# A fused attention, MLP and gated-MLP kernel: the loads of the q and k sums on GpSimd's queue, their decay pieces made early, the low half of v on GpSimd, one subtraction of the mean, and a block's stores on GpSimd's queue

## The chip, the cores and the metric

The kernel runs as one program on one core of a Trainium2 chip. The metric is the device time of one execution in microseconds (us); lower is better.

## What is computed

Three stages follow each other: causal attention with a decay, an MLP behind a layer norm, and an MLP with a spatial gate. Batch 4, 8 heads, 576 positions, head size 64, model width 512, all in float32 at the interface.

```python
def _attn_ref(q, k, v, f):
    scores = scale * np.matmul(q, k.transpose(0, 1, 3, 2))
    cum = np.cumsum(np.log(np.clip(f, 0.0001, 1.0)), axis=-1)
    decay = cum[:, :, :, None] - cum[:, :, None, :]
    scores = np.where(causal, -1000000000.0, scores + decay)
    scores = scores - np.max(scores, axis=-1, keepdims=True)
    attn = np.exp(scores)
    attn = attn / (np.sum(attn, axis=-1, keepdims=True) + 1e-09)
    return np.matmul(attn, v)

def _moe_ref(x, g_ln, w_ch1, w_ch2):
    mu = np.mean(x, axis=-1, keepdims=True)
    var = np.mean((x - mu) ** 2, axis=-1, keepdims=True)
    xn = (x - mu) / np.sqrt(var + 1e-06) * g_ln
    return x + np.maximum(xn @ w_ch1, 0.0) @ w_ch2

def _moe2_ref(x, w_in, w_spatial, b_spatial, w_out):
    h = np.maximum(x @ w_in, 0.0)
    u, v = h[..., :512], h[..., 512:]
    v_n = layer_norm(v)
    v_s = np.einsum('ts,bsd->btd', w_spatial, v_n) + b_spatial[None, :, None]
    return (u * v_s) @ w_out
```

## The kernel before

**Blocks.** The 576 positions of each of the 4 batch rows are cut into queries 0 to 127 (`attention32`, two batch rows at a time, float32), 128 to 255 (`attention1`, also two at a time) and 256 to 575 (`attention`, one row at a time). `BLOCKS` lists the eight pieces in the order in which they are made; each gives a tile xT of 512 features by 256 positions, and a ninth tile collects the last 64 positions of each row. Each tile goes through `prep` (the attention, a store of xT to the DRAM tensor x2_d, and `norm`) and then through `mlp`, whose output is added onto x2_d by GpSimd DMAs that accumulate (L779). From about 624 us on only the third stage (`mlp2`) is left.

**Two halves.** After the first block matmuls take float16 pairs: a number times a power of two is split into a high half h (a rounded copy, made by ScalarE) and a low half l (the remainder, made by VectorE), and a product takes three matmuls. `make16` splits the MLP's weights (L637, L640), `parts16` the values v (L220, L221), `operands` q and k (L318), `mlp` the hidden layer (L754, L758).

**The sums of q and k.** The scale of q and of k in `attention` comes from the sums of their squares. `qknorm` makes them: eight tiles qs, two buffers, each filled by two DMAs on SyncE's queue of 64 partitions each (L268), VectorE squares and sums the q half (L271) and ScalarE the k half (L272). After the last tile a matmul adds over partitions (L275), and a dozen small steps give the scales. Then GpSimd writes the rows that carry the decay into the score matmul: minus eight times the running sum `cum` of the log decay as three float16 pieces each for queries and keys, with rows of a constant `one` beside them (L286 to L293), and one DMA stores them to decay_d (L294). `operands` loads six rows of it for each head (L313).

```
268  nc.sync.dma_start(out=t[64 * u : 64 * u + 64], in_=self.qk[b, h + u : h + 4 : 2, :64]...)
271  nc.vector.tensor_tensor_reduce(out=q, in0=q, in1=q, ...)
272  nc.scalar.activation(k, k, AF.Square, accum_out=ss[:, 1, i : i + 1])
```

**The norm of a block.** `norm` gets the mean of xT by a matmul and subtracts it, one VectorE instruction for each of four feature tiles (L664); it squares on ScalarE (L667), adds the four tiles on GpSimd (L671, L672) and takes their mean by a matmul (L650). From the second block on the subtraction writes xT in place, so it also waits until the store of xT (L1116, on SyncE's queue) has read it.

**What sets the order.** `run` gives every step of every generator a time on a common scale (`events`; the sums stand at `QKS` + `QKN` times i) and calls them in that order. The framework's scheduler then places the instructions on each engine, in a fixed order. An engine runs its own in that order, and a queue issues its DMAs in that order: one that waits holds up all behind it on the same queue.

## Time and profile before

| | us |
|---|---|
| median of 3 runs (821.86 to 824.97) | 823.38 |
| the profiled execution's own time | 820.29 |
| its span, first to last instruction | 818.5 |
| PE (TensorE matmul) busy | 771.9 |
| DVE (VectorE) busy | 568.6 |
| ACT (ScalarE) busy | 527.9 |
| POOL (GpSimd) busy | 86.4 |

The granted TensorE clock was 0.967 of full over the span. Lnnn is a line of the kernel before. "a<-b" is an instruction that writes tile a from tile b; xN counts instructions. An arrow with "DMA qs<-in_qk_dram" in the chain is the time from the issue of that transfer to its landing. SPq is SyncE's queue, which issues most DMAs. Windows are counted from the first instruction.

### The profile page before, as it was taken

To read this page: it belongs to the slowest core of one execution; us is meant where nothing else is said; L and a number is where in the kernel's file an instruction comes from. 1 tells how busy PE (TensorE), PEld (TensorE's weight loads), DVE (VectorE), ACT (ScalarE), POOL (GpSimd) and SP (SyncE) were. 2 spreads that over 40 slices of the span, in tenths; PEclk is the share of its full clock that TensorE was granted. 3 is DMA by queue.
4 is the path that set the end of the run, shared out by engine and by line. 5 is a ranking of instruction groups with operands and counts; after the bars stand their busy time and mean duration, and the time that the engine had idled before them with its cause. 6 is when DMAs were issued, how large, how long until landed. Compare 5 with 4: busy or idle time off the path is not lost.

```text
span 818.5 us, 16434 instructions
## 1 busy us (share of the span) xinstructions
PE 771.9 (94%) x5980; PEld 572.0 (70%) x5980; DVE 568.6 (69%) x1513; ACT 527.9 (64%) x1328; POOL 86.4 (11%) x128
## 2 busy tenths in 40 slices
PE   8899998985898999699999999999999899999998
PEld 7588886874676777377777878744447667768676
DVE  4699599646459999987995984688534573654634
ACT  4787488646638898887885883567325634656543
POOL 2000015001021212301021020100012000000000
PEclk8999999997799999799999999999999999999999
DMA  8789574489967899987796586552005230000101
GB/s 255 204 301 319 171 185 72 66 194 205 215 164 181 170 176 243 189 172 181 147 206 145 122 147 129 171 163 86 1 14 109 66 117 1 30 30 1 59 1 58
DMA packets 166628, 111.84 MB, mean 137 GB/s; under 512 B 106498, under 2 KB 151874, under 8 KB 166516
## 3 DMA queue, kind: packets, MB, share of 16 engines
q1 hardware_dynamic: 160280, 103.86, 52.8%
q0 software_dynamic: 5264, 5.16, 4.7%
q10 hardware_dynamic: 1004, 1.78, 0.8%
q8 instruction: 47, 0.77, 0.4%
q14 instruction: 33, 0.27, 0.1%
HBM read 71.60 MB, written 14.99 MB: 106 GB/s over the span
## 4 chain that ended last, share of the span: by engine, by line
PE 53%; DVE 17%; DMA 14%; issue 7%; ACT 7%; SPq 1%; POOL 0%; DVEq 0%; ACTq 0%; POOLq 0%
PE ph L747 11%; PE acc L732 10%; PE pb L687 8%; PE pb L689 8%; PE pb L688 8%; DMA qs<-in_qk_dram 5%; DVE wt L640 2%; DVE x L318 2%; DMA PT<-P 2%; DVE P L356 2%; DVE sd L339 2%; PE s L732 1%; DMA vr<-in_v_dram 1%; PE av L499 1%; DMA qk<-in_qk_dram 1%
## 5 line engine op out<-in xcount | busy, mean ns | idle before, releaser
L732 PE MATMUL acc<-hh,wt 128*128 128x256 f16 (+2 forms) x960 | 197.9, 298 | 2.3 <-ACT hh L754 2.1
L747 PE MATMUL ph<-xh,wt 128*128 128x256 f16 (+1 forms) x896 | 189.2, 293 | 9.6 <-DVE hl L758 5.1
L747 PEld LDWEIGHTS <-wt 128*128 128x128 f16 x1344 | 131.2, 100 | 59.4 <-issue 16.7
L732 PEld LDWEIGHTS <-wt 128*128 128x128 f16 x1344 | 132.1, 99 | 45.6 <-issue 4.8
L747 PE MATMUL ph<-xl,wt 128*128 128x256 f16 (+1 forms) x448 | 131.1, 293 | 0.0
L732 PE MATMUL acc<-hl,wt 128*128 128x256 f16 (+1 forms) x416 | 116.7, 284 | 0.0
L754 ACT ACTIVATE hh<-ph 128x256 f16<-128x256 f32 (+2 forms) x128 | 50.9, 398 | 51.8 <-PE ph L747 51.5
L298 ACT ACTIVATE P<-sd,st 128x512 f16<-128x512 f32 (+2 forms) x128 | 70.6, 585 | 11.3 <-DVE st L346 10.3
L758 DVE SCALAR_TENSOR_TENSOR hl<-ph,hh 128x256 f16<-128x256 f32 (+1 forms) x112 | 50.4, 453 | 33.0 <-ACT hh L754 32.7
L343 ACT ACTIVATE sd<-sd,st 128x384 f32<-128x384 f32 (+2 forms) x80 | 54.6, 682 | 19.3 <-DVE st L339 18.8
L356 DVE SCALAR_TENSOR_TENSOR P<-sd,st,P 128x384 f16<-128x384 f32 (+2 forms) x96 | 59.1, 634 | 9.6 <-ACT P L298 9.4
L339 DVE CUSTOM_DVE_ANT_0 sd<-s,mask,qkneg 128x384 f32<-128x384 f32 (+2 forms) x80 | 50.7, 639 | 4.5 <-PE s L335 2.9
L335 PE MATMUL s<-x 128*64 128x288 f16 (+5 forms) x256 | 47.6, 330 | 4.5 <-DVE st L339 3.5
L779 POOL DMA_DIRECT2D x_d<-t x36 | 32.5, 1101 | 182.8 <-DVE t L775 151.2
L318 DVE SCALAR_TENSOR_TENSOR x<-qk,qksc,x 64x320 f16<-64x320 f32 x64 | 45.9, 717 | 2.9 <-ACT x L298 1.4
L298 ACT ACTIVATE x<-qk,qksc 128x320 f16<-128x320 f32 x64 | 38.0, 655 | 3.5 <-PE s L335 2.4
L1030 DVE SCALAR_TENSOR_TENSOR u<-pb,wsc,u 128x288 f32<-128x288 f32 x32 | 15.9, 514 | 34.2 <-PE pb L1029 34.2
L689 PE MATMUL pb<-x2h,wih 128*128 128x288 f16 (+2 forms) x144 | 37.8, 273 | 0.0
L688 PE MATMUL pb<-x2l,wih 128*128 128x288 f16 (+2 forms) x144 | 37.8, 273 | 0.0
L687 PE MATMUL pb<-x2h,wil 128*128 128x288 f16 (+2 forms) x144 | 37.8, 273 | 0.0
L687 PE MATMUL pb<-wsh,vl 128*128 128x288 f16 x128 | 36.6, 286 | 0.2 <-DVE x2s L201 0.2
L689 PE MATMUL pb<-wsh,vh 128*128 128x288 f16 x128 | 36.6, 286 | 0.0
(297 smaller groups left out, 1632.2 us busy)
## 6 DMA issues: line engine op xcount, KB each, us to landing
raw<-in_moe_w_ch_dram SPq DMA_DIRECT2D x32, 512.0 KB
qk<-in_qk_dram SPq DMA_DIRECT2D x32, 448.0 KB
qs<-in_qk_dram SPq DMA_DIRECT2D x16, 448.0 KB
vraw<-in_v_dram SPq DMA_DIRECT2D x5, 1024.0 KB
vr<-in_v_dram SPq DMA_DIRECT2D x16, 320.0 KB
x_d<-xT SPq DMA_DIRECT2D x9, 512.0 KB
x_d<-t POOLq DMA_DIRECT2D x36, 128.0 KB, 4.9
out_dram<-o SPq DMA_DIRECT2D x32, 144.0 KB
```

What stands on the lines that cost most here:

```text
L298: self.nc.scalar.activation(out, in_, AF.Copy, scale=scale)
L318: nc.vector.scalar_tensor_tensor(out=t, in0=qk[r, c], scalar=(sk if c.start else sq)[r], in1=x, op0=ALU.mult, op1=ALU.subtract)
L339: nc.vector.tensor_tensor_reduce(out=sd[:M, c0:c1], in0=ps[:M, : c1 - c0], in1=mask, scale=self.qkneg[:M], scalar=3e38 if n == 0 else st[: ...
L343: nc.scalar.activation(sd[:M, :N], sd[:M, :N], AF.Exp, bias=st[:M, n : n + 1], scale=-1.0, accum_out=st[:M, 2:3])
L356: low = nc.vector.scalar_tensor_tensor(out=dl, in0=src, scalar=rs, in1=dh, op0=ALU.mult, op1=ALU.subtract)
L687: first = mm(out, lhsT=al, rhs=bh, start=start, stop=False, **kw)
L688: mm(out, lhsT=ah, rhs=bl, start=False, stop=False, **kw)
L689: mm(out, lhsT=ah, rhs=bh, start=False, stop=stop, **kw)
L732: ins = nc.tensor.matmul(acc[m], lhsT=a, rhs=b, start=bank not in clear, stop=last and e == len(terms) - 1, skip_group_check=True)
L747: ins = nc.tensor.matmul(ph, lhsT=a, rhs=b, start=k == e == 0, stop=k == NK - 1 and e == len(terms) - 1)
L754: relu = nc.scalar.activation(hh, ph, AF.Relu)
L758: nc.vector.scalar_tensor_tensor(out=hl, in0=ph, scalar=0.0, in1=hh, op0=ALU.max, op1=ALU.subtract)
```

## The change

Five edits in one.

- **Sums' loads.** `qknorm` takes eight tiles of a pool of their own with four buffers. One DMA fills a tile, on GpSimd's queue and over all 128 partitions: `pair_of` views the two stored copies of each head so that the second copy of one head and the first of the next stand in 128 consecutive rows. The first four loads are placed at time `QKL` = 0.98, the squares at `QKS` = 1.325 and after (before: loads and squares from 1.12 on); a square is kept behind the last VectorE instruction of `make16` (`marks["made"]`). A later load is issued once the square of the tile four before is made.
- **Decay pieces.** `decays`, at the start of the program, makes the six rows from `cum` and stores them with two GpSimd DMAs. After the sums only the rows of the constant are left: one GpSimd instruction and two DMAs.
- **Low half of v.** In `attention`, and there alone, `parts16` scales vr in place on GpSimd and subtracts h there (`spare`), in place of one VectorE instruction.
- **Mean.** `norm` subtracts the mean in one VectorE instruction over all four tiles, the mean read with a broadcast.
- **Stores.** The store of xT to x2_d goes to GpSimd's queue.

```diff
-QKS, QKN = 1.12, 0.025
+QKL, QKS, QKN = 0.98, 1.325, 0.008
+QKB = 4
...
@@ decays @@
-        cum = self.cum = self.cst.tile([n, S], F32, name="cum")
+        cum = wk.tile([n, S], F32, name="cum")
+        rows = wk.tile([n, 6, S], F16, name="rows")
...
         nc.gpsimd.dma_start(out=self.decay1_d, in_=dec1)
+        nc.gpsimd.tensor_scalar(out=one, in0=cum, scalar1=-8.0, scalar2=1.0, op0=ALU.mult, op1=ALU.mult)
+        for i in range(3):
+            self.copy(1, rows[:, 3 + i], one)
+            if i < 2:
+                nc.gpsimd.tensor_tensor(out=one, in0=one, in1=rows[:, 3 + i], op=ALU.subtract)
+        self.copy(1, rows[:, :3], rows[:, 3:], -1.0)
+        nc.gpsimd.dma_start(out=self.decay_d[:, :3, :QW], in_=rows[:, :3, 2 * P :])
+        nc.gpsimd.dma_start(out=self.decay_d[:, 3:, QW:], in_=rows[:, 3:])
...
@@ parts16 @@
         nc.scalar.activation(h, v, AF.Copy, scale=scale)
-        nc.vector.scalar_tensor_tensor(out=l, in0=v, scalar=scale, in1=h, op0=ALU.mult, op1=ALU.subtract)
+        if spare:
+            self.copy(1, v, v, scale)
+            nc.gpsimd.tensor_tensor(out=l, in0=v, in1=h, op=ALU.subtract)
+        else:
+            nc.vector.scalar_tensor_tensor(out=l, in0=v, scalar=scale, in1=h, op0=ALU.mult, op1=ALU.subtract)
...
@@ qknorm @@
-        n = B * H // 4
+        n = B * NP // 2
+        cm = self.pool("qs")
+        qs = cm.__enter__()
...
+        def load():
+            i = len(tiles)
+            tiles.append(qs.tile([P, 2, C], F32, tag="qs", name="qs", bufs=QKB))
+            b, p = i * 2 // NP, i * 2 % NP
+            nc.gpsimd.dma_start(out=tiles[i], in_=self.pair_of(b)[p : p + 2].rearrange("p r s -> r p s"))
+
+        for i in range(QKB):
+            load()
+        yield
         for i in range(n):
-            t = at.tile([P, 2, C], F32, tag="qs", name="qs", bufs=2)
-            b, h = i * 4 // H, i * 4 % H
-            for u in range(2):
-                nc.sync.dma_start(out=t[64 * u : 64 * u + 64], in_=self.qk[b, h + u : h + 4 : 2, :64].rearrange("p d s -> d p s"))
+            q, k = tiles[i][:, :, :W], tiles[i][:, :, W:]
+            for ins in (nc.vector.tensor_tensor_reduce(out=q, in0=q, in1=q, ...),
+                        nc.scalar.activation(k, k, AF.Square, ...)):
+                self.after(ins, self.marks["made"])
+            if len(tiles) < n:
+                load()
             yield
-            q, k = t[:, :, :W], t[:, :, W:]
-            nc.vector.tensor_tensor_reduce(out=q, in0=q, in1=q, ...)
-            nc.scalar.activation(k, k, AF.Square, ...)
...
         gp, m = nc.gpsimd, B * H
-        c = one[:m]
-        rows = at.tile([m, 6, C], F16, name="drows", bufs=1)
...
-        gp.dma_start(out=self.decay_d, in_=rows)
+        rows = qs.tile([m, 3, S], F16, tag="rows", name="rows", bufs=1)
+        gp.memset(rows, 0.0)
+        gp.tensor_scalar(out=rows, in0=rows, scalar1=one[:m], scalar2=1.0, op0=ALU.add, op1=ALU.mult)
+        gp.dma_start(out=self.decay_d[:, :3, W:], in_=rows)
+        gp.dma_start(out=self.decay_d[:, 3:, :W], in_=rows[:, :, :W])
+        cm.__exit__(None, None, None)
...
+    def pair_of(self, b):
+
+        return self.qk[b].rearrange("(p u) (v d) s -> p (u v d) s", p=NP, v=2)[:, D : 3 * D]
...
@@ attention @@
-            vsc = self.parts16(vr, vp[:, 0], vp[:, 1], b)
+            vsc = self.parts16(vr, vp[:, 0], vp[:, 1], b, True)
...
@@ make16 @@
-            nc.vector.scalar_tensor_tensor(out=l[:, c], in0=src[:, c], ...)
+            self.marks["made"] = nc.vector.scalar_tensor_tensor(out=l[:, c], in0=src[:, c], ...)
...
@@ norm @@
-        for t in range(NK):
-            nc.vector.tensor_tensor(out=c[:, t, :], in0=x[:, t, :], in1=pm, op=ALU.subtract)
+        nc.vector.tensor_tensor(out=c, in0=x, in1=pm.unsqueeze(1).broadcast_to([P, NK, TOK]), op=ALU.subtract)
...
@@ run, prep @@
-            self.nc.sync.dma_start(out=self.rows(self.x2_d, n), in_=xT)
+            self.nc.gpsimd.dma_start(out=self.rows(self.x2_d, n), in_=xT)
...
-        events += [(QKS + QKN * i, -3, i) for i in range(B * H // 4 + 1)]
+        events += [(QKL, -3, 0)] + [(QKS + QKN * i, -3, i + 1) for i in range(B * NP // 2 + 1)]
```

The scheduler reorders around these edits; three places show what the prediction speaks of. In the changed kernel lines are some 20 further on: L1139 is the store of xT, L286 the load of a qs tile, L293 the square of its q half, L664 and L781 the VectorE lines of `make16` and of the hidden layer, L694 and L695 the GpSimd adds of a norm.

**Queues at the sums.** SyncE's queue before, from the store of the third block's xT on; L439 to L441 load the operands of `attention1` for the fourth:

```order
L1116 DMA x_d<-xT 128x4x256
L439 DMA qk<-in_qk_dram 64x768
L440 DMA qk<-decay_d 2x2x384
L441 DMA vr<-in_v_dram 128x2x128
L268 DMA qs<-in_qk_dram 64x2x896 x2
L439 DMA qk<-in_qk_dram 64x768
L440 DMA qk<-decay_d 2x2x384
L441 DMA vr<-in_v_dram 128x2x128
L268 DMA qs<-in_qk_dram 64x2x896 x2
L439 DMA qk<-in_qk_dram 64x768
L440 DMA qk<-decay_d 2x2x384
L268 DMA qs<-in_qk_dram 64x2x896 x2
```

GpSimd's queue with the change, from the first block's store on:

```order
L1139 DMA x_d<-xT 128x4x256
L694 TENSOR_TENSOR sq<-sq 128x512
L695 TENSOR_TENSOR sq<-sq 128x256
L286 DMA qs<-in_qk_dram 128x2x896 x4
L310 MEMSET rows 32x1728
L1139 DMA x_d<-xT 128x4x256
L694 TENSOR_TENSOR sq<-sq 128x512
L695 TENSOR_TENSOR sq<-sq 128x256
L802 DMA x_d<-t 128x256 x4
L286 DMA qs<-in_qk_dram 128x2x896 x4
L1139 DMA x_d<-xT 128x4x256
L694 TENSOR_TENSOR sq<-sq 128x512
```

The loads of qs have left SyncE's queue. Four now stand ahead of the second block's store and norm on GpSimd's, four behind the accumulates of the first MLP (L802) and ahead of the third block's store.

**VectorE at the sums.** Before, squares stand between the score steps (L451) and the low half of the hidden layer (L758) of the fourth block's stretch:

```order
L758 SCALAR_TENSOR_TENSOR hl<-ph,hh 128x256
L221 SCALAR_TENSOR_TENSOR vp<-vr,vsc,vp 128x256
L455 RECIPROCAL st<-st 128x2
L271 ISA qs,qkss<-qs 128x2x320
L271 ISA qkss 128x1
L451 ISA sd,st<-s,mask 128x256
L451 ISA st 128x1
L451 ISA sd,st<-s,mask 128x256
L451 ISA st 128x1
L462 SCALAR_TENSOR_TENSOR P_1689<-sd,st,P_1689 128x2x128 x2
L758 SCALAR_TENSOR_TENSOR hl<-ph,hh 128x256
L271 ISA qs,qkss<-qs 128x2x320
```

With the change the first four stand right behind the last two instructions of `make16`:

```order
L664 SCALAR_TENSOR_TENSOR wt<-wt,w1c 128x512
L664 SCALAR_TENSOR_TENSOR wt<-wt,w2c 128x512
L212 TENSOR_SCALAR vs<-vs 128x1
L293 ISA qs,qkss<-qs 128x2x320
L293 ISA qkss 128x1
L293 ISA qs,qkss<-qs 128x2x320
L293 ISA qkss 128x1
L781 SCALAR_TENSOR_TENSOR hl<-ph,hh 128x256
L293 ISA qs,qkss<-qs 128x2x320
L293 ISA qkss 128x1
L293 ISA qs,qkss<-qs 128x2x320
L293 ISA qkss 128x1
```

Three of the other four stand some 20 rows on, the last six rows behind them:

```order
L293 ISA qs,qkss<-qs 128x2x320
L293 ISA qkss 128x1
L781 SCALAR_TENSOR_TENSOR hl<-ph,hh 128x256
L235 SCALAR_TENSOR_TENSOR vp<-vr,vs,vp 128x256
L293 ISA qs,qkss<-qs 128x2x320
L293 ISA qkss 128x1
L479 RECIPROCAL st<-st 128x2 x2
L781 SCALAR_TENSOR_TENSOR hl<-ph,hh 128x256
L293 ISA qs,qkss<-qs 128x2x320
L293 ISA qkss 128x1
```

All eight squares have moved from the fourth block's `attention1` to the end of the third's; the last four are spread among the hidden layer's low halves, which TensorE waits for.

**GpSimd in `attention`.** Before, in the fifth block (x<-x is the copy of half of an operand that `operands` makes, L300, and MEMSET P clears padding):

```order
L350 MEMSET P_2880 128x2x64
L779 DMA x_d<-t 128x256 x4
L300 TENSOR_SCALAR x_3178<-x_3177 64x320
L350 MEMSET P_3164 128x2x64
L300 TENSOR_SCALAR x_3570<-x_3569 64x320
L300 TENSOR_SCALAR x_3581<-x_3580 64x320
L300 TENSOR_SCALAR x_3670<-x_3669 64x320
```

With the change, at the same place:

```order
L320 TENSOR_SCALAR vr<-vr,vsc 128x640
L233 TENSOR_TENSOR vp<-vr,vp 128x640
L802 DMA x_d<-t 128x256 x2
L320 TENSOR_SCALAR x_3168<-x_3167 64x320
L320 TENSOR_SCALAR x_3558<-x_3557 64x320
L802 DMA x_d<-t 128x256 x2
L374 MEMSET P_3153 128x2x64
L320 TENSOR_SCALAR vr<-vr,vsc 128x640
L233 TENSOR_TENSOR vp<-vr,vp 128x640
```

Two instructions on vr have come ahead of the accumulates and of the copies; there are sixteen such pairs in the program.

## Rows read from the trace of the kernel before

**Rows 1.** The page, part 4: the chain that ended last, by line.

```profile
PE ph L747 11%; PE acc L732 10%; PE pb L687 8%; PE pb L689 8%; PE pb L688 8%; DMA qs<-in_qk_dram 5%; DVE wt L640 2%; DVE x L318 2%; DMA PT<-P 2%; DVE P L356 2%; DVE sd L339 2%; PE s L732 1%; DMA vr<-in_v_dram 1%; PE av L499 1%; DMA qk<-in_qk_dram 1%
```

**Rows 2.** Four stretches: length, PE, PEld, DVE, ACT, POOL busy (count), clock, DMA, GB/s.

```profile
...
100.00:140.00 40.00, 36.28 (x278) 30.36 (x277) 38.54 (x99) 34.69 (x89) 13.74 (x13) 0.96 0.68 143
140.00:168.00 28.00, 27.94 (x285) 23.61 (x286) 17.94 (x59) 17.23 (x55) 0.00 (x0) 1.00 0.35 66
168.00:228.00 60.00, 45.02 (x301) 33.34 (x299) 32.54 (x106) 35.99 (x100) 5.55 (x6) 0.80 1.06 206
...
240.00:330.00 90.00, 86.79 (x788) 66.89 (x786) 83.22 (x214) 76.08 (x195) 17.15 (x29) 1.00 0.93 196
...
```

**Rows 3.** The chain in order of time, 140 to 250 us (start, length, what).

```profile
...
166.03 0.37 SPq L1116
...
169.02 6.78 DMA qs<-in_qk_dram
...
177.81 9.55 DMA qs<-in_qk_dram
...
189.52 11.90 DMA qs<-in_qk_dram
...
204.12 7.99 DMA qs<-in_qk_dram
...
217.81 6.57 DMA qs<-in_qk_dram
...
```

**Rows 4.** Waits, 168 to 228 us (total, times, longest).

```profile
...
DVE qs L271 <- DMA qs<-in_qk_dram: 23.1, 8, 4.4
ACT qs L272 <- DMA qs<-in_qk_dram: 16.3, 8, 3.6
...
```

**Rows 5.** Instructions on tile qs alone: length, DVE busy, ACT busy, clock, DMA, GB/s.

```profile
168.00:228.00 60.00, 6.61 (x8) 10.06 (x16) 0.80 1.06 206
```

**Rows 6.** The chain in order of time: a 448 KB load onto 128 partitions.

```profile
275.48 4.59 DMA qk<-in_qk_dram
```

**Rows 7.** DVE groups by form, 119.8 to 126.9 us: count, busy us, mean ns.

```profile
L640 DVE SCALAR_TENSOR_TENSOR wt<-wt,w1c 128x512 f16<-128x512 f32 x4 | 3.0, 744 | 0.0
L640 DVE SCALAR_TENSOR_TENSOR wt<-wt,w2c 128x512 f16<-128x512 f32 x3 | 2.2, 746 | 0.0
```

**Rows 8.** The same two groups, 126.9 to 134.3 us.

```profile
L640 DVE SCALAR_TENSOR_TENSOR wt<-wt,w1c 128x512 f16<-128x512 f32 x3 | 3.5, 1157 | 0.0
L640 DVE SCALAR_TENSOR_TENSOR wt<-wt,w2c 128x512 f16<-128x512 f32 x3 | 3.3, 1100 | 0.0
```

**Rows 9.** POOL alone, 126.9 to 135.3 us: length, busy, clock, DMA, GB/s.

```profile
126.90:135.30 8.40, 7.83 (x7) 0.85 0.35 69
```

**Rows 10.** POOL groups by form over the whole run.

```profile
...
L290 POOL TENSOR_TENSOR dcum<-dcum,drows 32x576 f32<-32x576 f32 x2 | 2.9, 1432 | 0.2
...
L286 POOL TENSOR_SCALAR dcum<-cum 32x576 f32<-32x576 f32 x1 | 0.7, 696 | 0.1
...
```

**Rows 11.** DVE groups by form over the whole run.

```profile
...
L221 DVE SCALAR_TENSOR_TENSOR vp<-vr,vsc,vp 128x640 f16<-128x640 f32 x16 | 14.2, 890 | 2.1 <-ACT vp L220 1.9
...
L664 DVE TENSOR_TENSOR xT<-xT,av 128x256 f32<-128x256 f32 x28 | 9.9, 413 | 4.9 <-DMA x_d<-xT 2.6 <-PE ph L747 2.1
...
L681 DVE TENSOR_TENSOR xT<-xT,y 128x1024 f32<-128x1024 f32 x8 | 9.7, 1216 | 0.0
...
L664 DVE TENSOR_TENSOR xT<-xT,s 128x256 f32<-128x256 f32 x8 | 2.8, 416 | 1.6 <-PE s L650 0.8 <-DMA x_d<-xT 0.8
...
```

**Rows 12.** Tile x_d: duration ns min/median/max, first and last start; landing.

```profile
...
L779 POOL DMA_DIRECT2D x_d<-t x36: 858/905/1738, 122.5 to 622.8; - x36
...
DMA to landing us min/median/max: 3.0/4.9/8.1
```

**Rows 13.** The chain in order of time at the end of the fifth block.

```profile
...
316.69 4.92 DMA x_d<-xT
...
```

**Rows 14.** Timeline, 323 to 343 us: GpSimd add of the squares, and its idle time.

```profile
...
324.32 1.69 POOL L671 TENSOR_TENSOR sq<-sq 128x512 f32<-128x512 f32 x1 [9.13 <-ACT sq L667]
...
```

More of the change, by code (lines that the diff above doesn't have):

```diff
@@ L263, in qknorm @@
         self.qkneg = self.cst.tile([P, 1], F32, name="qkneg")
[L264 to L268 removed]
+        tiles = []
+        def load():
[6 more added lines that the diff above has]
+        yield
+        for i in range(n):
+            q, k = tiles[i][:, :, :W], tiles[i][:, :, W:]
+            for ins in (nc.vector.tensor_tensor_reduce(out=q, in0=q, in1=q, scale=1.0, scalar=0.0, op0=ALU.mult, op1=ALU.add, accum_out=ss[:, 0, i : i + 1]),
+                        nc.scalar.activation(k, k, AF.Square, accum_out=ss[:, 1, i : i + 1])):
+                self.after(ins, self.marks["made"])
+            if len(tiles) < n:
+                load()
             yield
[L270 to L272 removed]
         nc.vector.tensor_reduce(out=tot, in_=ss, axis=mybir.AxisListType.X, op=ALU.add)
@@ L282, in qknorm @@
         gp, m = nc.gpsimd, B * H
-        c = one[:m]
-        rows = at.tile([m, 6, C], F16, name="drows", bufs=1)
-        t = at.tile([m, S], F32, name="dcum", bufs=1)
-        gp.tensor_scalar(out=t, in0=self.cum, scalar1=-8.0, scalar2=1.0, op0=ALU.mult, op1=ALU.mult)
-        for i in range(3):
-            self.copy(1, rows[:, 3 + i, W:], t)
-            if i < 2:
-                gp.tensor_tensor(out=t, in0=t, in1=rows[:, 3 + i, W:], op=ALU.subtract)
-        self.copy(1, rows[:, :3, :W], rows[:, 3:, W + 2 * P :], -1.0)
-        gp.tensor_scalar(out=rows[:, :3, W:], in0=rows[:, 3:, W:], scalar1=0.0, scalar2=c, op0=ALU.mult, op1=ALU.add)
-        gp.tensor_scalar(out=rows[:, 3:, :W], in0=rows[:, :3, :W], scalar1=0.0, scalar2=c, op0=ALU.mult, op1=ALU.add)
-        gp.dma_start(out=self.decay_d, in_=rows)
+        rows = qs.tile([m, 3, S], F16, tag="rows", name="rows", bufs=1)
[4 more added lines that the diff above has]
+        cm.__exit__(None, None, None)
     def copy(self, e, out, in_, scale=1.0):
@@ L639, in make16 @@
                 self.after(ins, self.xh)
-            nc.vector.scalar_tensor_tensor(out=l[:, c], in0=src[:, c], scalar=sc, in1=h[:, c], op0=ALU.mult, op1=ALU.subtract)
+            self.marks["made"] = nc.vector.scalar_tensor_tensor(out=l[:, c], in0=src[:, c], scalar=sc, in1=h[:, c], op0=ALU.mult, op1=ALU.subtract)
     def pair(self, j):
```

6 lines of the change are left out of this document (2 added, 4 removed).

## The prediction

> **What bounds the kernel now.** I read the page's busy table first: TensorE is busy for 771.9 of 818.5 us, so a gain must come from a place where TensorE waits or crawls. The chain that ended last is the second view [rows 1]. Matmul lines fill most of it; among the rest one entry is larger than every other, 5% of the span for the landing of qs, the loads for the sums of q and k. The third view, busy time by stretch, shows where [rows 2]. From 140 to 168 us TensorE makes 285 matmuls in 28 us at full clock, 10.2 per us, and this is the pace at which it has no gaps. From 168 to 228 us it makes 301 in 60 us, at a mean granted clock of 0.80 of full. At the earlier pace these take 301 / 10.2 = 29.6 us, so this stretch loses 60 - 29.6 = 30.4 us. Neither VectorE (32.5 of 60) nor ScalarE (36.0) is full there, but the DMA engines are (share 1.06, against 0.35 just before).
>
> The chain in order of time names the mechanism [rows 3]. At 166.03 the SyncE queue issues the third block's store, and from 169.02 on five landings of qs follow each other, 6.78 + 9.55 + 11.90 + 7.99 + 6.57 = 42.8 us of the 60. With two buffers a load waits for a square, and the square, in VectorE's and ScalarE's fixed order, holds up the low halves that TensorE needs. The waits agree: eight of VectorE for 23.1 us and eight of ScalarE for 16.3 [rows 4]. In 240 to 330 us the limits differ: VectorE is busy for 83.2 of 90 us and TensorE for 86.8 [rows 2], so there both are close to the bound.
>
> **The change, part by part.** The sum is made against the profiled execution, 820.29 us; the median of the runs shown is 3.1 us above it.
>
> *1. The stall goes.* The eight loads leave the stretch, and its loss of 30.4 us is the most that can come back: -30.4. The squares go too, 6.61 us of VectorE and 10.06 of ScalarE [rows 5]. They move mostly into 140 to 168 us, where VectorE has 10.1 and ScalarE 10.8 us free [rows 2]; this is their cover, and without it they would cost up to 10 us.
>
> *2. What is late next there.* The fourth block's `attention1` remains: 32.54 - 6.61 = 25.9 us of VectorE and 35.99 - 10.06 = 25.9 us of ScalarE, feeding each other. If they overlap fully, TensorE's 29.6 us bound the stretch, and nothing is given back. If they alternate strictly, it lasts 51.9 us, and 22 are given back. From 100 to 140 us the same two engines do 38.5 and 34.7 us of work in 40 [rows 2], so they overlap well; I am nearer the good end and take +10 (0 to 22).
>
> *3. The loads at their new place.* They are 8 x 896 KB = 7.3 MB. At the 206 GB/s of the full stretch that is 36 us of all engines; free are 0.32 x 40 + 0.65 x 28 = 31 us between 100 and 168 [rows 2], so they almost fit. The first four can land before about 140 us, when `make16` ends. The last four can only be issued behind the first squares, some 18 us of transfers into 65% free engines, so the last may land 27 us later, while the order wants it after about six steps of the hidden layer, 6 x 24 / 10.2 = 14 us. The wait lies between 0 and 13 us. One load is twice the 448 KB that took 4.59 us on 128 partitions [rows 6], about 9 us, against some 4 us of VectorE work between the fourth square and the fifth; I take +5. GpSimd's part is cheap: it is idle from 140 to 168 us [rows 2], and an issue of 128 rows costs it 0.9 us [rows 12].
>
> *4. Decay pieces.* GpSimd worked for 7.83 us between 126.9 and 135.3 us [rows 9], in a stretch in which VectorE is busy for 38.5 of 40. The low halves of `make16`, 744 and 746 ns just before [rows 7], took 1157 and 1100 ns beside it [rows 8]: 3 x 0.413 + 3 x 0.354 = 2.3 us lost, or 0.29 us of VectorE per us of GpSimd. At the program's start GpSimd has nothing else to do and the rows are not needed until after 228 us, so this is free there: -2 (-3 to 0).
>
> *5. Low half of v.* VectorE loses sixteen instructions, 14.2 us [rows 11]. GpSimd gets sixteen pairs; by the nearest rows, 1432 and 696 ns for 576 columns [rows 10], a pair of 640 columns costs 2.13 x 640 / 576 = 2.36 us, together 37.8. GpSimd has the time (17.2 of 90 us busy [rows 2]), and the product with v comes a pair of heads later, so 1.5 us more of delay is hidden. The price is contention: 0.29 x 37.8 = 11 us of VectorE, bounded by 0 and 37.8. The Trainium skill, page "SBUF — State Buffer", section "Who interferes with whom", says that a VectorE instruction with two SBUF inputs and a GpSimd instruction that reads SBUF exclude each other, and that the loser blocks fully. Taken at its hardest this charges all 37.8 us; rows 7 to 9 show the effect, at 0.29.
>
> *6. One subtraction.* 36 instructions, 9.9 + 2.8 us, become nine of 1024 columns. The nearest is the 1216 ns of the product of the same size [rows 11]: 9 x 1.22 = 10.9, a gain of 1.8 us. Parts 5 and 6 change VectorE by -14.2 + 11 - 1.8 = -5 us (-16 to +22). TensorE is at 96% there, so I count nothing: 0 (-4 to +22).
>
> *7. Stores.* On GpSimd a store has 512 rows, by 0.9 us for 128 rows between 0.9 and 3.6 us, nine times. The adds of the same block stand behind it; in the fifth block they began at 324.32 [rows 14], 7.6 us after the store's issue at 316.69 [rows 13], and this covers it. The in-place subtraction waits for the store to be read: 4.92 us there [rows 13], against 3.0 to 8.1 for GpSimd's quarter-sized accumulates [rows 12]. What is queued behind a late store or a late vr on GpSimd is the operand copy of a next head. I take +1 (-2 to +6).
>
> Sum: -30.4 + 10 + 5 - 2 + 0 + 1 = -16.4, so 803.9 us for an execution like the profiled one and **807 us** for the median.
>
> **Rivals.** *Late squares.* Parts 1 and 2 go as I say, but the last four loads land at the bad end, +13 instead of +5. For it speaks that they share the DMA engines with the fourth block's operands; against it that those engines are at 0.35 before 168 us. That gives 815 us.
>
> *Nothing won.* The stretch is then held by VectorE and ScalarE alternating, +22, with a wait of 7 us for the squares: -30.4 + 22 + 7 - 2 + 1 = -2.4, 821 us. The DMA bytes do not change, and from 100 to 228 us the engines have 0.68 x 40 + 0.35 x 28 + 1.06 x 60 = 101 of 128 us to do already. The Trainium skill, page "DMA: Bandwidth & Descriptors", section "Issuing engines are not separate DMA queues", says that another queue saves only the time of issuing, since all share the same sixteen engines. By that rule alone the new queue wins nothing and only the earlier start counts; no row here shows two queues loading at once.
>
> *GpSimd blocks VectorE.* The place is 240 to 480 us, the price up to 1 us of VectorE per us of GpSimd: 37.8 - 16 = +22 on an engine that is 92% busy, 807 + 22 = 829 us, slower than before. It decides above (16.4 + 16) / 37.8 = 0.86. For it speaks that VectorE there mostly runs instructions of two SBUF inputs; against it the 0.29 of rows 7 to 9, measured beside such instructions too.
>
> **How the numbers follow.** About 0.5%, 4 us, is what a measurement of this kernel can tell from no change. The forecast has 0.61 and its own range is 795 to 817 us; late squares 0.12, faster as well; nothing won 0.14; GpSimd blocking 0.13. So faster has 0.73, the same 0.14, slower 0.13. The range reaches from 794, about halfway from the sum to its good ends in parts 2 to 7, to 824, which takes in late squares and nothing won; outside are GpSimd blocking and some 0.05 below.
>
> **What would show it.** Right: no landing of qs on the chain for more than some 8 us together; the matmuls that now run from 168 to 228 us done in some 40 to 47 us at a clock near full; landings of the last four loads before 170 us. Low halves of v and operand copies on GpSimd should leave the mean of VectorE's `P` and `x` lines (L356, L318) up by under a tenth. Wrong: a wait of VectorE for qs of over 10 us, VectorE's two-input lines up by a fifth or more between 240 and 480 us, or a norm that waits for GpSimd's store.

## The result and the profile after

The changed kernel takes 831.16 us (median of 5 runs, 828.85 to 833.09) against 823.38 for the kernel before: ratio 1.0088, 95% interval 1.0066 to 1.0111. It is slower, and the prediction of 807 us, with a range to 824, was wrong. The profiled execution took 831.16 us, its span is 829.4 us (before 818.5), and the granted TensorE clock was 0.969.

Line numbers of the changed kernel are 10 to 14 higher in `parts16` and 18 to 24 higher from `qknorm` on: L380 is the `P` line (before L356), L342 the `x` line (L318), L486 the `P` of `attention1` (L462), L495 its product with v (L471), L687 the mean subtraction (L664), L781 the hidden layer's low half (L758).

Busy time by stretch after the change; columns as in [rows 2]:

```profile
20.00:40.00 20.00, 14.62 (x77) 10.70 (x77) 11.72 (x24) 14.46 (x29) 3.50 (x4) 0.84 0.74 191
40.00:100.00 60.00, 58.94 (x383) 50.24 (x381) 47.58 (x81) 40.89 (x82) 3.99 (x4) 0.99 0.93 323
100.00:140.00 40.00, 35.63 (x256) 29.70 (x254) 30.06 (x91) 28.20 (x76) 6.37 (x7) 0.91 0.61 160
140.00:168.00 28.00, 25.56 (x231) 21.93 (x232) 24.86 (x71) 27.49 (x71) 2.97 (x4) 1.00 0.39 111
168.00:228.00 60.00, 42.58 (x377) 33.51 (x375) 33.91 (x112) 32.74 (x100) 9.53 (x10) 0.86 0.81 136
228.00:240.00 12.00, 12.00 (x124) 10.22 (x122) 5.78 (x10) 5.61 (x12) 2.54 (x4) 1.00 0.65 223
240.00:330.00 90.00, 85.08 (x760) 64.62 (x758) 84.09 (x206) 75.57 (x197) 30.49 (x39) 1.00 0.87 180
330.00:360.00 30.00, 26.43 (x265) 19.62 (x264) 29.15 (x77) 24.75 (x66) 10.66 (x14) 1.00 1.02 174
360.00:480.00 120.00, 113.10 (x1036) 89.48 (x1034) 97.69 (x230) 86.94 (x227) 36.15 (x45) 0.99 0.74 153
480.00:530.00 50.00, 47.55 (x425) 38.72 (x425) 30.05 (x74) 25.78 (x65) 6.10 (x9) 0.97 0.64 138
```

Three stretches of the kernel before that [rows 2] leaves out:

```profile
330.00:360.00 30.00, 21.88 (x183) 14.55 (x182) 28.32 (x73) 25.44 (x67) 6.92 (x10) 0.77 0.92 174
360.00:480.00 120.00, 117.06 (x1097) 92.31 (x1094) 102.90 (x265) 92.09 (x243) 20.57 (x32) 1.00 0.78 164
480.00:530.00 50.00, 50.00 (x459) 41.07 (x458) 29.87 (x78) 25.39 (x61) 1.59 (x4) 1.00 0.65 151
```

TensorE's matmuls, the counts in the first brackets, tell where the time went. (They are of unequal lengths, so 10 to the microsecond is rough.) In 168 to 228 us it makes 377 where it made 301: part of the old stall is gone. But from 100 to 168 it makes 487 where it made 563, and these 76 cancel those 76. From 240 to 330 it makes 28 fewer; from 330 to 360, 82 more (a stall of the kernel before is gone there); from 360 to 530, 95 fewer. By 240 us the changed kernel has made 1448 since 20 us and the old one 1481, 33 more: nothing is won there, and more is lost after 360.

The stall between 168 and 228 us has become one idle time. First what TensorE did (start, length, what, in brackets the idle time before it and what ended it), then the waits from 168 to 228 us:

```profile
170.58 0.27 PE L755 MATMUL acc<-hh,wt 128*128 128x256 f16 x1
181.42 0.85 PE L495 MATMUL av<-PT,vp 128*64 128x128 f16 x12 [10.56 <-DMA PT<-P]
```

```profile
POOL x_d L1139 <- ACT xT L496: 26.7, 1, 26.7
...
PE av L495 <- DMA PT<-P: 11.4, 2, 10.6
...
DVE qs L293 <- DMA qs<-in_qk_dram: 6.0, 2, 4.7
```

TensorE waits for a transposed P, that is, for a DMA, and not for a square. VectorE's waits for qs are down from 23.1 us [rows 4] to 6.0. The last four loads were issued between 158.72 and 164.61 us, behind squares that came after the last weight of `make16` (156.8 us).

After 240 us two VectorE groups are slower and GpSimd has new ones (page, part 5, and the groups by line from 230 to 530 us; busy us, mean ns, idle time before):

```profile
L380 DVE SCALAR_TENSOR_TENSOR P<-sd,st,P 128x384 f16<-128x384 f32 (+2 forms) x96 | 66.9, 718 | 16.3 <-ACT P L318 15.9
L342 DVE SCALAR_TENSOR_TENSOR x<-qk,qksc,x 64x320 f16<-64x320 f32 x64 | 49.9, 779 | 1.7
```

```profile
L233 POOL TENSOR_TENSOR vp<-vr,vp 128x640 f16<-128x640 f32 x16 | 24.8, 1552 | 1.1
...
L320 POOL TENSOR_SCALAR vr<-vr,vsc 128x640 f32<-128x640 f32 x16 | 13.7, 854 | 52.7 <-ACT st L369 24.0 <-ACT vp L230 20.6 <-PE ph L770 5.2
```

Before, `P` took 634 ns and `x` 717. GpSimd's pair takes 1.55 + 0.85 = 2.41 us (2.36 were forecast), and its queue stands still for 52.7 us in front of the scaling.

### The profile page after: what moved, and what is told of

Read it like the earlier page. It is cut to its first block, busy times and chain, and to the rows that moved or that the text cites. A ratio compares the mean times of both kernels' runs of the same rounds, so it can differ in the third digit from the quotient of the medians.

```text
span 829.4 us, 16441 instructions
## 1 busy us (share of the span) xinstructions
PE 769.7 (93%) x5980; PEld 572.4 (69%) x5980; DVE 568.9 (69%) x1470; ACT 527.4 (64%) x1328; POOL 137.1 (17%) x180
## 5 line engine op out<-in xcount | busy, mean ns | idle before, releaser
L318 ACT ACTIVATE P<-sd,st 128x512 f16<-128x512 f32 (+2 forms) x128 | 70.4, 585 | 16.2 <-DVE st L370 7.2
L380 DVE SCALAR_TENSOR_TENSOR P<-sd,st,P 128x384 f16<-128x384 f32 (+2 forms) x96 | 66.9, 718 | 16.3 <-ACT P L318 15.9
L781 DVE SCALAR_TENSOR_TENSOR hl<-ph,hh 128x256 f16<-128x256 f32 (+1 forms) x112 | 50.4, 452 | 35.4 <-ACT hh L777 35.3
L802 POOL DMA_DIRECT2D x_d<-t x36 | 33.7, 1089 | 122.5 <-DVE t L798 102.7
L342 DVE SCALAR_TENSOR_TENSOR x<-qk,qksc,x 64x320 f16<-64x320 f32 x64 | 49.9, 779 | 1.7
L770 PE MATMUL ph<-xg,wt 128*128 128x256 f32 x128 | 34.4, 404 | 5.0 <-ACT xg L734 4.6
L318 ACT ACTIVATE x<-qk,qksc 128x320 f16<-128x320 f32 x64 | 37.7, 655 | 1.4 <-PE s L359 1.4
L523 PE MATMUL av<-PT,vp 128*64 128x320 f16 (+2 forms) x480 | 32.3, 270 | 5.6 <-DMA PT<-P 4.8
```

Source lines behind the costliest of these rows:

```text
L318: self.nc.scalar.activation(out, in_, AF.Copy, scale=scale)
L342: nc.vector.scalar_tensor_tensor(out=t, in0=qk[r, c], scalar=(sk if c.start else sq)[r], in1=x, op0=ALU.mult, op1=ALU.subtract)
L380: low = nc.vector.scalar_tensor_tensor(out=dl, in0=src, scalar=rs, in1=dh, op0=ALU.mult, op1=ALU.subtract)
L770: ins = nc.tensor.matmul(ph, lhsT=a, rhs=b, start=k == e == 0, stop=k == NK - 1 and e == len(terms) - 1)
L781: nc.vector.scalar_tensor_tensor(out=hl, in0=ph, scalar=0.0, in1=hh, op0=ALU.max, op1=ALU.subtract)
```

## Experiments

Each kernel was timed beside the kernel before; the ratio is to that. "Loads alone" is the kernel before with the sums' loads and the early decay pieces of the change.

| label | what it is | us | ratio (95%) |
|---|---|---|---|
| u_store | changed, stores back on SyncE | 827.61 | 1.0045 (1.0023, 1.0066) |
| u_v | changed, low half of v back on VectorE | 816.58 | 0.9924 (0.9900, 0.9948) |
| u_sub | changed, four subtractions | 820.41 | 0.9952 (0.9933, 0.9972) |
| loads_alone | loads and decay pieces only | 802.12 | 0.9744 (0.9724, 0.9764) |
| l_sub | loads alone + one subtraction | 812.95 | 0.9878 (0.9839, 0.9918) |
| l_store | loads alone + stores on GpSimd | 812.90 | 0.9875 (0.9852, 0.9899) |
| l_v | loads alone + low half of v on GpSimd | 821.38 | 0.9979 (0.9956, 1.0001) |
| a_nosq | changed, last four squares left out | 833.08 | 1.0117 (1.0089, 1.0145) |
| l_dummy | loads alone + GpSimd pairs that serve nothing | 823.18 | 1.0019 (0.9994, 1.0043) |
| l_vfree | l_v, the pair fed from tiles of its own | 806.92 | 0.9821 (0.9798, 0.9843) |
| l_early | loads alone, squares early | 799.39 | 0.9732 (0.9694, 0.9770) |
| e_sub | l_early + one subtraction | 808.43 | 0.9811 (0.9796, 0.9827) |
| e_store | l_early + stores on GpSimd | 808.20 | 0.9818 (0.9789, 0.9848) |
| a_early | changed, squares early | 818.17 | 0.9935 (0.9912, 0.9957) |
| e_two | l_early, two subtractions | 808.30 | 0.9843 (0.9798, 0.9887) |
| e_rev | l_early, four in reverse sequence | 802.44 | 0.9757 (0.9725, 0.9790) |
| b_decay | before + early decay pieces | 821.91 | 1.0011 (0.9988, 1.0035) |
| b_shape | before, loads over 128 partitions | 812.42 | 0.9905 (0.9876, 0.9935) |

### Which part costs

```diff
u_store:  -nc.gpsimd.dma_start(out=self.rows(self.x2_d, n), in_=xT)
          +nc.sync.dma_start(out=self.rows(self.x2_d, n), in_=xT)
u_v:      -vsc = self.parts16(vr, vp[:, 0], vp[:, 1], b, True)
          +vsc = self.parts16(vr, vp[:, 0], vp[:, 1], b)
u_sub:    -nc.vector.tensor_tensor(out=c, in0=x, in1=pm.unsqueeze(1).broadcast_to(...), op=ALU.subtract)
          +for t in range(NK):
          +    nc.vector.tensor_tensor(out=c[:, t, :], in0=x[:, t, :], in1=pm, op=ALU.subtract)
loads_alone: all three
```

> The changed kernel with the stores of a block's attention output back on SyncE's queue; everything else as changed. Theory A (the store stands in GpSimd's queue among the loads, so the second block's mean subtraction slid from 102.4 us to 116.8, the last weights from about 145 to 157 us, and with them the squares and the last four loads; this made TensorE's idle time of 10.6 us at 170 to 181): the subtraction starts before 106 us again, the first square before 148, the idle time is under 4 us, and the time is 815 to 821. Theory B (the loads come in two halves and the second half is late wherever the store is): the idle time stays at 7 to 11 us and the time is 827 to 832. Theory C (GpSimd's new work on v slows VectorE after 240 us): says nothing of the stretch before 240 us, and expects the loss of about 9 us between 240 and 530 us to stay.

> The changed kernel with the low half of v back on VectorE; everything else as changed. Theory C (GpSimd's work beside VectorE's two-input instructions costs more than the 14.2 us it takes off VectorE): the means of the lines that make P and x fall from 718 and 779 ns back to 630 to 650 and 715 to 730, and the time is 820 to 824. Rival to C (VectorE's loss and gain cancel, and the loss after 240 us is GpSimd's order: copies and stores wait behind v): the means fall the same, the time is 826 to 829. Theories A and B: nothing changes before 230 us, the idle time at 170 to 181 stays.

> The changed kernel with the mean subtracted in four instructions again; everything else as changed. All theories: 830 to 834, at most 2 us slower than the changed kernel. If a single subtraction that waits for the whole mean and the whole store were what holds the norms, it would be faster, under 827.

> The kernel before with only the new loads for the sums on GpSimd's queue, in two halves of four, and the decay pieces made early; the stores, the low half of v and the subtractions are as before. Theory A: the stretch from 140 to 240 us gains what the prediction gave it, 805 to 812. Theory B: TensorE still stands idle for 7 to 11 us before the last squares, 816 to 822. If parts 1 and 4 win nothing by themselves: 822 to 826.

The loads and the decay pieces alone give 802.12 us, 21 us less than before, 5 less than my forecast for the whole, and below every range that I gave this run. The other three edits cost 29 us together; undoing one gives back 3.5, 14.6 and 10.7. In u_sub the theories expected nothing; what came is the alternative named beside them, under 827. Theory A was half right. With the stores on SyncE the last four loads go out from 148.1 us instead of 158.7, but TensorE's idle time stays (8.4 us, ended by PT again) only 13 us earlier, as theory B says. In loads_alone no wait for PT there is longer than 1.7 us. For the low half of v the two lines fell about as theory C said (`P` 627 ns, `x` 742, both just outside its ranges), with a larger gain than it said (816.58 against 820 to 824).

Then one edit at a time on top of the loads:

> The new loads and early decay pieces (802.1 us by themselves) and, of the other three edits, the single subtraction alone. Additive costs (each edit costs what undoing it gave back: 3.5 for the stores, 10.7 for the subtraction, 14.6 for the low half of v; their sum, 28.8, is the whole distance from 802.1 to 831.2): 812 to 814. Theory D (the subtraction itself costs nothing; it moves the order so that a transpose of P by DMA is in flight together with the last loads for the sums, and both crawl; in the changed kernel the DMA engines then moved about 100 GB/s at a full share): between 802 and 813, and the excess over 802 stands as idle time of TensorE between 150 and 175 us, in front of a product that waits for PT.

> The new loads and early decay pieces and, of the other three edits, the stores on GpSimd's queue alone. Additive costs: 805 to 806.5. Theory A (a store behind loads moves the second block's norm and the squares by 10 us): the first square at 155 to 160 us instead of 147, the second block's subtraction after 110 us, and the time is 804 to 812.

> The new loads and early decay pieces and, of the other three edits, the low half of v on GpSimd alone. Additive costs: 815 to 818. Theory C (contention: undoing it took 37.4 us of GpSimd and left VectorE 3.1 us less busy although it got 14.2 us of work back, so 17.3 / 37.4 = 0.46 us of VectorE per us of GpSimd): VectorE's P line back at 690 to 730 ns against 627, its x line at 760 to 790 against 706, the loss lies after 240 us, and the time is 810 to 818. If the loss came from the order of the other edits: 801 to 805.

They cost 10.8, 10.8 and 19.3 us. The sum, 40.9, is more than the 29.0 that they cost together: they overlap. In l_sub TensorE waits 9.9 us for a PT, from 160.5 to 170.4 us, as theory D says; the time alone would fit additive costs too. l_v is slower than both of its ranges, and its lines are above theory C's (`P` 737 ns, `x` 806). In l_store the last loads go out from 160.6 us, as theory A says, without one long wait (812.9 us, just above its range).

### What the last loads meet

a_nosq is the changed kernel with the last four loads made and their squares left out:

```diff
-for ins in (nc.vector.tensor_tensor_reduce(...), nc.scalar.activation(k, k, AF.Square, ...)):
+for ins in () if i >= QKB else (nc.vector.tensor_tensor_reduce(...), nc.scalar.activation(k, k, AF.Square, ...)):
```

> The changed kernel, in which the last four loads for the sums are made as before but their squares are left out (the sums take in the first four loads alone). Theory D (the transposes of P and the last loads slow each other): TensorE's idle time of about 10 us near 175 us stays, 6 us or more, and while the two overlap the DMA engines move under 200 GB/s at a share over 0.9; 825 to 831. Rival, theory E (VectorE's fixed order: the squares that wait for the loads hold up P, 4.7 us, and the rest follows from it): with no square behind these loads the idle time is under 3 us and the time is 817 to 823.

The idle time stays, and the time is 833.1 us, above the range of theory D, so VectorE's sequence (theory E) is not its cause. TensorE's long wait in a_nosq from 155 to 190 us, and the busy times by 5 us (the last three numbers of a row are clock, DMA share and GB/s):

```profile
PE av L495 <- DMA PT<-P: 10.9, 1, 10.9
```

```profile
160.00:165.00 5.00, 4.55 (x42) 3.92 (x41) 3.75 (x21) 5.00 (x19) 1.96 (x3) 1.00 0.99 348
165.00:170.00 5.00, 5.00 (x48) 4.47 (x47) 2.21 (x7) 1.67 (x6) 0.00 (x0) 1.00 1.32 252
170.00:175.00 5.00, 0.65 (x6) 0.33 (x4) 0.00 (x0) 0.00 (x0) 0.00 (x0) 0.81 1.04 128
175.00:180.00 5.00, 0.00 (x0) 0.00 (x0) 0.00 (x0) 0.00 (x0) 0.00 (x0) 0.50 1.18 73
```

The loads begin at 348 GB/s. Once transposes are in flight with them, the DMA engines are at a full share and move 73 to 128. The same stretch of the changed kernel, then the stretch of loads_alone in which its last loads run:

```profile
170.00:175.00 5.00, 0.85 (x8) 0.52 (x6) 1.81 (x5) 1.26 (x2) 0.00 (x0) 0.99 1.26 89
175.00:180.00 5.00, 0.00 (x0) 0.00 (x0) 0.15 (x1) 0.00 (x0) 0.00 (x0) 0.50 0.96 122
```

```profile
155.00:160.00 5.00, 5.00 (x48) 4.47 (x46) 4.62 (x19) 4.25 (x14) 0.00 (x0) 1.00 1.00 375
160.00:165.00 5.00, 4.50 (x49) 3.66 (x47) 3.50 (x12) 5.00 (x15) 0.00 (x0) 1.00 0.80 106
```

In loads_alone the first transpose that meets these loads is issued at 155.21 and the last load has landed by 162.1, so the two are in flight together for 6.9 us at most. The queues tell it as well. From 150 to 170 us, first u_store, then loads_alone (queue, packets, MB, share; q0 carries the loads, q1 mostly the transposes, in u_store one load of 128 KB as well):

```profile
q0 software_dynamic: 557, 3.55, 61.1%
q1 hardware_dynamic: 1784, 0.51, 50.3%
```

```profile
q0 software_dynamic: 562, 3.57, 46.2%
q1 hardware_dynamic: 3693, 0.92, 37.9%
```

A packet of q1 costs 50.3% of 16 x 20 us / 1784 = 90 ns in u_store, 33 ns in loads_alone. a_nosq shows it within one run. From 145 to 155 us transposes alone are in flight (but for one packet of another queue), from 170 to 180 transposes and loads:

```profile
q1 hardware_dynamic: 2112, 0.52, 27.3%
```

```profile
q1 hardware_dynamic: 983, 0.25, 77.4%
q0 software_dynamic: 119, 0.76, 33.7%
```

By the same sum a transpose's packet takes 21 ns alone and 126 ns beside loads. So loads and transposes in flight together slow each other: that is shown. Why they do so no row here tells. The Trainium skill, page "SBUF — State Buffer", section "Who interferes with whom", has another reason for a stalled DMA of GpSimd's queue: a VectorE instruction that holds the port which GpSimd needs to write the descriptors. It is not that here, since VectorE is busy for 0.00 us from 170 to 180 us in a_nosq.

### The low half of v: contention or waiting

```diff
l_dummy:  vsc = self.parts16(vr, vp[:, 0], vp[:, 1], b)
         +self.copy(1, d32, d32, vsc)
         +nc.gpsimd.tensor_tensor(out=d16[:, 1], in0=d32, in1=d16[:, 0], op=ALU.subtract)
l_vfree:  the same two, out=vp[:, 1] in the second, and no low half on VectorE
```

> The new loads and early decay pieces (802.1 us), with the low half of v on VectorE as before, and beside it on GpSimd sixteen pairs of instructions of the same shapes as the low half's (a scaling of 640 columns and a subtraction), on a tile of their own; they wait for no other engine's work and nobody waits for them. The low half on GpSimd cost 19.3 us. Theory C (contention, 0.44 us of VectorE per us of GpSimd): VectorE's P line at 700 to 740 ns, its x line over 760, VectorE busy for 14 to 18 us more than with the loads alone, and the time is 812 to 825, since nothing is taken off VectorE here. Rival, theory F (the loss is waiting: GpSimd's queue stands still for ScalarE's high half, 82 us in all, and operand copies wait behind it): the P line rises as well, but the time is 802 to 808.

> The new loads and early decay pieces; VectorE's sixteen low halves of v are left out, and GpSimd writes that half from tiles of its own, in two instructions of the same shapes that do not wait for ScalarE's high half or for the load of v. So the low half of v is not computed here. GpSimd's work by itself, beside a VectorE that keeps its low halves, cost 21 us; the real low half on GpSimd costs 19.3 although it takes 14.2 us off VectorE. Theory C (only VectorE's busy time counts): 21 less 14, 805 to 811. Theory F (what counts is also that the queue waits for ScalarE and operand copies wait behind it): the same, since the waits are gone here, while the real low half cost 10 to 14 us more for its waits. If it comes out at 816 to 823 instead, the busy time taken off VectorE is worth nothing there and the price is the longer single instruction in each chain.

The first row of the page for loads_alone, l_v, l_dummy and l_vfree, in this order:

```profile
PE 765.5 (96%) x5980; PEld 570.4 (71%) x5980; DVE 566.6 (71%) x1513; ACT 526.5 (66%) x1328; POOL 94.0 (12%) x139
```

```profile
PE 774.1 (94%) x5980; PEld 572.7 (70%) x5980; DVE 570.1 (69%) x1497; ACT 527.4 (64%) x1328; POOL 133.8 (16%) x171
```

```profile
PE 769.3 (94%) x5980; PEld 570.0 (70%) x5980; DVE 585.1 (71%) x1513; ACT 526.2 (64%) x1328; POOL 142.1 (17%) x179
```

```profile
PE 764.2 (95%) x5980; PEld 568.7 (71%) x5980; DVE 574.9 (71%) x1497; ACT 527.0 (65%) x1328; POOL 143.3 (18%) x179
```

In l_dummy 48.1 us more of GpSimd make VectorE 18.5 us busier: 0.38 us per us. In l_vfree it is 8.3 + 14.2 (the low halves that VectorE no longer makes) = 22.5 for 49.3, 0.46; in l_v 3.5 + 14.2 = 17.7 for 39.8, 0.44. This is contention, and with nothing taken off VectorE the pairs cost 21.1 us of time, so theory F alone is out. (In l_dummy the pairs bunch, as they wait for little: GpSimd is busy for 38.9 of the 60 us from 240 to 300 us, against 18.4 in l_v. The 21.1 us are their price at that place.)

But it is not what l_v costs: there VectorE is only 3.5 us busier, and the time is 19.3 longer. In l_vfree VectorE is 8.3 us busier, and the time is only 4.8 longer. What l_vfree lacks are the waits for ScalarE's high half and for the load of v, and GpSimd's work on vr. So about 14.5 of the 19.3 us go with these, and theory C does not cover them. (The three differ in the order of the program too, which by the next section can be worth some microseconds; the split is no finer than that.) The rows of l_v, 230 to 530 us:

```profile
L380 DVE SCALAR_TENSOR_TENSOR P<-sd,st,P 128x384 f16<-128x384 f32 (+2 forms) x96 | 68.7, 737 | 11.9 <-ACT P L318 11.2
```

```profile
L320 POOL TENSOR_SCALAR vr<-vr,vsc 128x640 f32<-128x640 f32 x15 | 13.3, 890 | 96.1 <-ACT vp L230 44.3 <-ACT st L369 37.9 <-issue 9.2
```

GpSimd's queue stands for 96 us in front of the scaling of v, and what is behind it in that queue (operand copies of later heads, sums of squares of the norm) stands too. But a standing queue is not yet a cost. In loads_alone it stands just as long, 96.4 us, in front of the operand copies, and in l_vfree the subtraction waits too, for TensorE to release vp:

```profile
L560 POOL TENSOR_TENSOR vp<-d,d 128x640 f16<-128x640 f32 x14 | 22.7, 1621 | 54.2 <-PE av L522 54.2
```

TensorE's own waits from 230 to 530 us add up to 7.8 us in loads_alone, 14.0 in l_vfree and 20.7 in l_v. Two of l_v:

```profile
PE s L359 <- DVE st L363: 7.9, 8, 2.4
...
PE s L359 <- POOL vr L320: 3.3, 1, 3.3
```

Little of this is a direct wait for GpSimd. There is also a rival to theory F that no run tests: vr has one buffer, and in l_v the next load of v waits four times, 7.5 us, until GpSimd's subtraction has read it; in loads_alone it waits once, 2.0 us, for VectorE's. So the 14.5 us are shown as the price of tying the pair to ScalarE, to the load and to vr; how it reaches TensorE stays open.

### Where the squares stand, and what an order costs

```diff
l_early, a_early, e_*: -QKL, QKS, QKN = 0.98, 1.325, 0.008
                       +QKL, QKS, QKN = 0.98, 1.0, 0.008
                       -self.after(ins, self.marks["made"])
e_sub, e_store:        the edit of l_sub, of l_store
```

> The new loads and early decay pieces, with the squares put before the last weights instead of behind them, so that the last four loads are issued between about 105 and 125 us. Theory D (loads and transposes of P in flight together slow each other): the first attention with transposes runs there too, so the collision moves to 105 to 135 us; TensorE, which still has other work there until 125, loses under 5 us, and the time is 798 to 806. If the late squares are what is left of the loss between 140 and 240 us: 792 to 798. If the 6.6 us of squares on a full VectorE before the last weights count fully: 806 to 810.

> Early squares (799.4 us) with the single subtraction. With late squares this edit cost 10.8 us, and TensorE stood idle from 158 to 168. Theory D (it cost that because the order let the last loads meet transposes of P): with the loads over by 135 us nothing is left to collide, 797 to 802. If the single subtraction costs by itself (a norm that waits for the whole sum): 806 to 811.

> Early squares (799.4 us) with the stores on GpSimd's queue. With late squares this edit cost 10.8 us: 7 of them before 240 us, without a single long idle time. Theory A (it cost that because a store behind the loads moved the second block's norm): the loads are still in that queue, so 804 to 811. If it cost only through the place of the squares: 798 to 803.

> The whole changed kernel (831.2 us) with early squares. Theory D: TensorE's idle time of 10.6 us at 170 to 181 us goes, and the loss after 240 us stays; 818 to 823. If the stores and the subtraction cost by themselves as well: 826 to 831.

With early squares the last loads are issued by 119.9 us, and no wait of TensorE for PT between 140 and 240 us is longer than 0.9 us. The changed kernel gains 13.0 us (a_early): the long idle time is gone, and the rest of the loss stays. Loads alone gain 2.7, to 799.39, the lowest median here; the intervals of the two overlap, so this gain is not shown.

Theory D alone would make the subtraction free now; it still costs 9.0 us. VectorE is busy for 566.0 us in e_sub and for 566.0 in l_early: the instruction itself costs nothing. For the stores theory A has the time (808.2 of 804 to 811) and the place. The second block's mean subtraction (start, length) in loads_alone, then in the changed kernel:

```profile
106.38 1.40 DVE L688 TENSOR_TENSOR xT<-xT,av 128x256 f32<-128x256 f32 x4
```

```profile
116.76 1.21 DVE L687 TENSOR_TENSOR xT<-xT,av 128x1024 f32<-128x1024 f32 x1
```

It starts at 107.0 in l_early and 106.2 in e_sub, both with stores on SyncE, and at 115.1 in e_store, 116.7 in l_store and 115.3 in u_sub, all with the stores behind the loads in GpSimd's queue. VectorE does not stand idle in front of it: it has its place that late in the sequence. Nor does the queue hold the store up: it is issued at 101.0 us in l_store and at 100.95 in loads_alone. So it is the order that the scheduler chose, not the store as it ran, that moved the norm; that this shift makes the whole 8.8 us is not shown.

Two more kernels on the subtraction:

```diff
e_two: +for t in (0, 2): subtract from x[:, t : t + 2, :]
e_rev: +for t in reversed(range(NK)): subtract from x[:, t, :]
```

> Early squares (799.4 us) with the mean subtracted in two instructions of 512 columns. One instruction cost 9.0 us, four are in the 799.4. Theory H (a wider subtraction costs by itself, since the norm starts later and holds VectorE longer): about half, 802 to 806. Theory I (the cost is that the program is ordered anew: with one instruction 69% of VectorE's instructions stand in the same sequence as with four, with two 76%): no relation to the width, anything from 797 to 812; outside 802 to 806 it speaks for I.

> Early squares (799.4 us) with the four subtractions in the reverse sequence; the work is the same to the last column. Theory H: no change, 798 to 801. Theory I (a new order by itself moves the time): 96% of VectorE's and 87% of TensorE's instructions stand in the same sequence here, so a smaller move than the 9.0 us of the single subtraction, but more than 2 us to either side.

Two instructions cost 8.9 us, as much as one, and outside the 802 to 806 of theory H; the reverse sequence of four equal instructions costs 3.0, but its interval and that of l_early overlap (0.9725 to 0.9790, 0.9694 to 0.9770). The first speaks against theory H and leans to theory I, that a new order of the program moves the time by itself; the second is too small to tell. It is not settled, since no edit leaves the order as it was, and no single wait carries the 9 us.

### Two parts by themselves

```diff
b_decay: the change's decay pieces, in the kernel before
b_shape: -for u in range(2): nc.sync.dma_start(out=t[64 * u : 64 * u + 64], in_=...)
         +nc.sync.dma_start(out=t, in_=<the change's view of 128 rows>)
```

> The kernel before with the decay pieces made early on GpSimd, nothing else. The prediction's part 4: 2 us faster, 820 to 823; GpSimd is idle between 126 and 135 us, and the low halves of the weights there take 745 ns again instead of up to 1157. If the rows' DMAs at the start delay the first block: 824 to 827. The rival that the order moves for other reasons: more than 4 us to either side.

> The kernel before with its loads for the sums at their old place and with two buffers, but each of them one transfer over 128 partitions on SyncE's queue in place of two over 64. Theory D: the stretch from 168 to 228 us stays bad, since loads and transposes of P are still in flight together; 818 to 824. Rival, theory G (the old loads were slow because each filled only 64 partitions): the five landings of 42.8 us halve, and the time is 802 to 812.

b_decay is no different from before (-1.0 to +2.9 us). The low halves of `make16` between 126.9 and 135.3 us take 750 ns, where they took 1157 and 1100 [rows 8]: the local gain came, and the time does not show it. b_shape gains 9.8 us, at the edge of theory G's range. So the old stall was in part the two loads of 64 partitions, or the order that came with one of 128, which this run does not part: on the chain from 160 to 240 us the landings of qs fall from 42.8 us to 24.5, VectorE's waits for qs from 160 to 230 us fall to 12.4 us there, and from 168 to 228 us its clock is 0.91, as in loads_alone, and its DMA share 0.93, between before (1.06) and loads_alone (0.74).

## Why the prediction was wrong

**Parts 1 to 4, the loads and the decay pieces: right in size.** Their sum was -30.4 + 10 + 5 - 2 = -17.4; loads_alone measured -21.4. That the two are so near is in part luck, as only part of the gain is where I put it. The rows of loads_alone:

```profile
140.00:168.00 28.00, 24.98 (x240) 20.99 (x241) 23.57 (x79) 24.89 (x70) 2.94 (x4) 1.00 0.69 191
168.00:228.00 60.00, 54.26 (x478) 42.97 (x477) 38.01 (x119) 34.74 (x102) 11.25 (x13) 0.91 0.74 154
...
330.00:360.00 30.00, 28.72 (x288) 22.40 (x289) 28.53 (x75) 26.30 (x72) 6.36 (x10) 1.00 1.04 204
```

From 168 to 228 us it makes 177 matmuls more than before, but in the stretches around it fewer; from 20 to 240 us it is 1558 to 1481, about 7.5 us at 10.2 per us (rough, as their lengths differ). From 330 to 360 us it makes 288 and the old one 183, another 10 us: an idle time of the kernel before, in which the hidden layer waits 4.5 us for ScalarE's xh and then runs at a low clock (0.77 in that row), is gone, and I had not forecast that. The -2 of part 4 did not come.

**Part 3, the loads' place.** The range of 0 to 13 us held, the mechanism did not: I shared out free DMA time and took a load for 9 us. Beside transposes of P one took up to 16.6 us, and the transposes were late as well; TensorE's 10.6 us came from these. The rival of late squares had the place and about the size, with the squares as the cause; a_nosq refutes that.

**Part 5, the low half of v: the step that failed most.** I counted -14.2 + 11 us on VectorE. The price per us of GpSimd was 0.38 to 0.46 where I took 0.29, so VectorE's net is +3.5 us. This was inside my bounds. By the Trainium skill, page "SBUF — State Buffer", section "Who interferes with whom", the ports that the two engines share are an exclusive lock; taken at its hardest that is 1.0, and the runs give less than half. What failed is the sentence that the delay is "hidden" because the product with v comes later, and with it the 0 that I set for parts 5 and 6: l_v measured +19.3, and some 14.5 of it went when the pair no longer hung on ScalarE's high half, the load of v and vr. The rival in which GpSimd blocks VectorE gave 829 us, near the 831 that came, but by a price above 0.86 that no run shows.

**Part 6, one subtraction: -1.8 forecast of VectorE and 0 of the time, +9.0 to +10.8 measured.** **Part 7, the stores: +1 forecast, +3.5 to +10.8 measured.** Both were priced by their own instructions and waits, and these do not hold the cost: VectorE's time is the same with the one (e_sub) and 3 us longer with the other (568.7 in e_store, 566.0 in l_early), and VectorE waited for a store three times, 6.8 us in all, in the changed kernel (3.4 before). The failed step is that the rest of the program was held fixed. The scheduler orders it anew: with the store behind the loads in the queue's order the second block's norm stands 10 us later in VectorE's sequence, and the single subtraction came with an order in which the loads met transposes (l_sub) or TensorE lost a few microseconds in several places (e_sub). What of the order makes the 9 us of the single subtraction stays open.

**What would show it.** Of my marks, three told the failure: the last two loads landed after 170 us (their squares start at 173.2 and 183.1), the `P` line is up by 13%, more than a tenth (`x` by 9%), and norms wait for GpSimd's store. The mark on VectorE's wait for qs (6.0 us, under my 10) looked like success, because the wait had gone to TensorE and PT.

## What to carry to other kernels

Five edits in one kernel hid a gain of 21 us behind 29 us of cost; time them one at a time. Work moved to an idle engine was not free where it hung on another engine's result and held a single buffer (19.3 us against 4.8 without): price these ties as well as the instruction. Where a scheduler orders the program, look at the sequence after the edit, and before you explain a cost of a percent that no wait shows, time a null edit, which changes the order alone.
